# Loads by head pair, merged constants and a masked bounds matrix in a fused attention and FFN kernel

## The chip, the cores and the metric

The kernel runs on one core of one Trainium2 chip. The metric is the device time of one execution in microseconds (us). Several executions were timed for each kernel, and each comparison uses executions of both kernels on the same chip.

The engines are named as the profile names them: PE is TensorE (matmuls; PEld is its weight load), DVE is VectorE, ACT is ScalarE, POOL is GpSimd and SP is SyncE. In this kernel nearly all DMA transfers that load inputs are issued by POOL, and the issuing instruction occupies POOL.

## The reference, cut to what matters

For each of 4 batches and 8 heads there are 768 positions with head size 64. The keys come in 24 chunks of 32. For each query, an upper bound of the score with each chunk is computed from the chunk's smallest and largest keys; the six chunks with the largest bounds are kept, the others are masked; then comes ordinary causal attention, and a feed-forward network (FFN) with squared ReLU on the joined heads.

```python
k_min = np.min(k_chunks, axis=3); k_max = np.max(k_chunks, axis=3)
ub = np.sum(np.maximum(q * k_min, q * k_max), axis=-1)   # one bound per query and chunk (axes cut)
ub = np.where(causal, ub, -1e9)
top_chunks = np.argsort(ub, axis=-1)[..., -6:]
scores = np.where(selected & causal_by_position, scale * (q @ k.T), -1e9)
attn = softmax(scores)
x = (attn @ v)  reshaped to (3072, 512)
h = np.maximum(x @ w_in, 0.0)        # w_in 512 x 2048
out = (h * h) @ w_out                # w_out 2048 x 512
```

## The kernel before

Heads are worked in pairs, four pairs to a batch. A batch is worked in two *phases*, each for a block of 384 queries; there are eight phases. In each phase PE interleaves the attention of that block with the FFN of an earlier block. The FFN of a block can finish its sums only when all four pairs have written their part of `xT`, so the first phase has hardly any FFN work to fill PE with.

For each pair, stage A makes the transposed keys and queries, the chunk bounds and the selection:

```python
def stage_a(p, halves):
    ...
    for nm in ("k", "q"):
        pt = pool.tile([128, nt * QB], BF16, tag=tag, name=nm + "T")
        ...                                   # transposes on PE: kn, qn -> kT, qT in PSUM
        ops = kq if nm == "k" else qs
        for hh in range(2):
            rows = slice(D * hh, D * hh + D)
            nc.vector.tensor_copy(ops[s][hh][0:D, cols], pt[rows])      # kqc, qsc
        if nm == "k":
            kr = work.tile([128, 2, NC // 2 * nt], BF16, tag="kr", name="kr")
            ...                               # two tensor_reduce: max and min of each chunk
            for hh in range(2):
                rows = slice(D * hh, D * hh + D)
                nc.vector.tensor_copy(
                    kbd[s][rows, :, hh, 12 * n0:12 * n1], kr[rows])     # block-diagonal
            yield
    nc.vector.tensor_scalar_max(qp[:, 0:m], pt[:, u0 - QB * n0:], 0.0)
    nc.vector.tensor_scalar_min(qm[:, 0:m], pt[:, u0 - QB * n0:], 0.0)
    yield
    yield from selection(p, HT * n0, HT * n1, qp, qm)   # ub (PE), max8, selb (DVE), sT (PE), qsc (DVE)
```

Stage B makes the scores `ps` (PE), the exponentials `e` (ACT), the causal mask of `e` (POOL) and the products with the values `av` (PE). It ends in a serial chain:

```python
def finish():
    av = hold.pop("av")                       # PSUM, one buffer for each head of a pair
    for hh in range(2):
        nc.scalar.activation(rc[...], av[hh][...], ACT.Ln)
    nc.scalar.activation(rc, rc, ACT.Exp, scale=-1.0)
    for hh in range(2):
        nc.vector.tensor_mul(xTs[tb][rows, hp], av[hh][rows], rc[rows])
    ...
    if left[tb] == 0:
        ffn.extend(ffn_units(tb))
```

The loads of the first batch are in many pieces (half a sequence, one pair or several); those of later batches are one block of 768 KB each for keys, queries and values:

```python
load_qk(0, 0, 2, (0,), "k")
ident = ...; make_identity(nc, ident)
load_qk(0, 0, 2, (0,), "q")
load_qk(0, 2, H, (0,))
... # constants
load_v(0, 0)
load_w_in(0, 4)
...
put(0, 1, L(load_qk, 0, 0, H, (1,)), L(load_w_in, 4, NFI))
put(0, 2, L(load_v, 0, 1))
...
put(1, 0, L(load_qk, 1, 0, H), L(load_w_out), L(load_v, 1))
```

`put(ph, i, ...)` places work in phase `ph` before the stage B of its pair `i`. It is the order in which the program is written; the order on each engine is settled when the program is built.

The softmax here doesn't subtract the row's maximum and nothing guards it: scores larger than these inputs give would overflow.

Of the kernel before, what the change touches and what calls it, by code (L numbers as in the profile page):

```python
# [9 lines left out]
F32 = mybir.dt.float32  # L10
BF16 = mybir.dt.bfloat16
# [7 lines left out]
def kernel(  # L19
# [23 lines left out]
    NEG = -32768.0  # L43
    NP = H // 2
# [20 lines left out]
    def load_qk(b, h0, h1, halves=(0, 1), what="kq"):  # L65

        for nm, src in (("k", k), ("q", q)):
            if nm not in what:
                continue
            if (nm, b) not in nat:  # L70
                nat[nm, b] = ld.tile([128, H, NT, D], BF16, tag=nm + "n",
                                     name=nm + "n")
            j0, j1 = HT * halves[0], HT * (halves[-1] + 1)
            if j1 - j0 == NT:
                nc.gpsimd.dma_start(
                    out=nat[nm, b][:, h0:h1].rearrange("p h j d -> p (h j) d"),
                    in_=src[b, h0:h1].rearrange("h (j p) d -> p (h j) d",
                                                p=128))
                continue
            if h1 - h0 <= j1 - j0:  # L80
                for h in range(h0, h1):
                    nc.gpsimd.dma_start(
                        out=nat[nm, b][:, h, j0:j1],
                        in_=src[b, h, 128 * j0:128 * j1].rearrange(
                            "(j p) d -> p j d", p=128))
                continue
            for j in range(j0, j1):
                nc.gpsimd.dma_start(
                    out=nat[nm, b][:, h0:h1, j],
                    in_=src[b, h0:h1, 128 * j:128 * (j + 1)].rearrange(  # L90
                        "h p d -> p h d"))
# [5 lines left out]
    def load_v(b, half=None):  # L97

        if half is None:
            nc.gpsimd.dma_start(  # L100
                out=vo[b % 2][:, :, :, 0:D].rearrange("p h j d -> p (h j) d"),
                in_=v[b].rearrange("h (j p) d -> p (h j) d", p=128))
            return
        for j in range(HT * half, HT * half + HT):
            nc.gpsimd.dma_start(
                out=vo[b % 2][:, :, j, 0:D],
                in_=v[b, :, 128 * j:128 * (j + 1)].rearrange("h p d -> p h d"))

    load_qk(0, 0, 2, (0,), "k")
    ident = consts.tile([128, 128], BF16, tag="ident")  # L110
    make_identity(nc, ident)
    load_qk(0, 0, 2, (0,), "q")
    load_qk(0, 2, H, (0,))
# [3 lines left out]
    kq, qs, kbd, selb = [], [], [], []  # L117
    for s in range(NSET):
        kq.append([consts.tile([KC, S], BF16, tag=f"kq{s}{hh}", name="kqc")
                   for hh in range(2)])  # L120
        qs.append([consts.tile([KC, S], BF16, tag=f"qs{s}{hh}", name="qsc")
                   for hh in range(2)])
        kbd.append(consts.tile([128, 2, 2, NC], BF16, tag=f"kbd{s}", name="kbd"))
        selb.append(consts.tile([128, NT, 2, 32], BF16, tag=f"selb{s}",
                                name="selb"))

    def set_constants(s):
        nc.vector.memset(kbd[s], 0.0)
        for hh in range(2):
            nc.vector.memset(qs[s][hh][D:KC, 0:128], 0.0)  # L130
        nc.vector.memset(selb[s][:, :, :, NC:], 0.0)
        nc.vector.memset(selb[s][:, NT - 1], 0.0)
        for hh in range(2):
            if (s, hh) == (0, 0):
                nc.scalar.activation(
                    kq[0][0][D:KC, :].rearrange("c (a j) -> c a j", j=CH),
# [346 lines left out]
```

## Time and profile before

| | before |
|---|---|
| median of 3 runs | 330.38 us (330.23 to 330.52) |
| profiled span | 328.7 us |
| last `xT` of the first phase done | 41.56 us |
| PE idle in the first phase | 17.86 us |
| PE idle in phases 2 to 4 | 7.72 us |
| PE idle in phases 5 to 8 | 8.52 us |

The idle times are the length of a stretch less PE's busy time, from the busy time by stretch. These are that view's lines for the kernel before. The columns are the stretch, its length, busy us of PE, PEld, DVE, ACT and POOL (in brackets the instructions), the granted clock, the DMA engines' share and GB/s (the share is printed as the view gives it, also where it is above 1; nothing here rests on it). The first line is the first phase, the second is phases 2 to 4, the third the rest.

```profile
0.00:41.56 41.56, 23.70 (x144) 11.57 (x145) 34.97 (x137) 18.54 (x40) 34.22 (x62) 1.00 1.44 135
41.56:167.46 125.90, 118.18 (x928) 63.65 (x938) 104.25 (x317) 86.89 (x219) 37.34 (x84) 1.00 0.90 80
167.46:328.70 161.24, 152.72 (x1005) 83.47 (x1013) 79.88 (x224) 112.74 (x282) 27.54 (x92) 1.00 0.15 32
```

After 41.56 us PE is busy 94% of the time.

These are lines of DVE's timeline (start, duration, engine, line, operation, what it writes and reads, shapes, how many, and in brackets the idle time before and what ended it):

```profile
5.85 2.11 DVE L410 MEMSET vo<- 128x512 bf16 x4
7.97 0.72 DVE L201 COPY kqc<-kT 64x384 bf16<-64x384 bf16 x2
...
35.22 1.78 DVE L211 COPY kbd<-kr 64x24 bf16<-64x24 bf16 x2
...
41.00 0.56 DVE L369 TENSOR_TENSOR xT<-av_647,rc 64x384 bf16<-64x384 f32 x1
```

Constants keep DVE until 7.97 us, when the first key copy starts. At 35.22 us two tiny copies into `kbd` take 1.78 us together. The timeline of POOL shows what ran beside them, the block issues for the second batch, and behind these the issue of `w_out`:

```profile
34.62 2.23 POOL L75 DMA_DIRECT2D kn<-in_k_dram  x1
36.84 2.23 POOL L75 DMA_DIRECT2D qn<-in_q_dram  x1
39.04 1.18 POOL L176 DMA_DIRECT2D w_out_sb<-in_moe_w_out_dram  x1
```

Lastly PE's timeline: the first value products of pairs 0, 1 and 3 and the start of pair 3's scores (`ps`).

```profile
18.70 0.53 PE L345 MATMUL av_395<-e,vo 128*128 128x384 bf16 x1
...
29.25 0.53 PE L345 MATMUL av_488<-e,vo 128*128 128x384 bf16 x1
...
31.41 1.01 PE L379 MATMUL ps<-qsc,kqc 88*128 88x384 bf16 x3 [0.46 <-DVE qsc L254]
...
37.63 0.82 PE L345 MATMUL av_646<-e,vo 128*128 128x384 bf16 x3 [1.77 <-DVE xT L369]
```

Followed back, the chain that ended last in this kernel does not run through the last `xT` of the first phase. It leaves that phase at 34.62 us, over the two block issues shown above, and goes on over the load of `w_out` to the first product that uses it, for which PE stood idle 0.43 us (start, duration, what):

```profile
39.04 21.04 DMA w_out_sb<-in_moe_w_out_dram
60.12 0.39 PE py L302
```

### The profile page before, as it was taken

To read this page: it belongs to the slowest core of one execution; us is meant where nothing else is said; L and a number is where in the kernel's file an instruction comes from. 1 tells how busy PE (TensorE), PEld (TensorE's weight loads), DVE (VectorE), ACT (ScalarE), POOL (GpSimd) and SP (SyncE) were. 2 spreads that over 40 slices of the span, in tenths; PEclk is the share of its full clock that TensorE was granted. 3 is DMA by queue.
4 is the path that set the end of the run, shared out by engine and by line. 5 is a ranking of instruction groups with operands and counts; after the bars stand their busy time and mean duration, and the time that the engine had idled before them with its cause. 6 is when DMAs were issued, how large, how long until landed. Compare 5 with 4: busy or idle time off the path is not lost.

```text
span 328.7 us, 6090 instructions
## 1 busy us (share of the span) xinstructions
PE 294.6 (90%) x2076; PEld 158.7 (48%) x2096; DVE 219.1 (67%) x678; ACT 218.2 (66%) x540; POOL 99.1 (30%) x237
## 2 busy tenths in 40 slices
PE   1397699999998999999999999999999999999995
PEld 1143344454454445555455455554555555554542
DVE  7987879778899867999485488994576213421420
ACT  6064556786666559887479766787579679973731
POOL 8886840452410722202142222111122311210000
PEclk9999999999999999999999999999999999999999
DMA  6999999999590891000193010000100000001001
GB/s 45 151 148 195 134 159 210 119 127 98 60 102 3 56 194 40 2 1 3 41 101 52 2 66 32 2 1 3 64 34 0 32 34 32 2 0 64 35 33 64
DMA packets 81371, 20.87 MB, mean 63 GB/s; under 512 B 74836, under 2 KB 77756, under 8 KB 81340
## 3 DMA queue, kind: packets, MB, share of 16 engines
q0 software_dynamic: 77344, 13.63, 53.8%
q1 hardware_dynamic: 3996, 6.85, 5.6%
q8 instruction: 16, 0.26, 0.3%
q14 instruction: 15, 0.12, 0.1%
HBM read 27.26 MB, written 6.29 MB: 102 GB/s over the span
## 4 chain that ended last, share of the span: by engine, by line
PE 55%; DVE 24%; ACT 8%; DMA 6%; issue 3%; POOL 2%; ACTq 0%; DVEq 0%
PE py L302 21%; PE ph L288 13%; PE ps L379 8%; DMA w_out_sb<-in_moe_w_out_dram 6%; DVE kr L206 4%; ACT rc L359 4%; DVE xT L369 3%; DVE qsc L201 3%; ACT e L383 2%; DVE kqc L201 2%; PE sT L249 2%; DVE qsc L254 1%; ACT rc L362 1%; PE kT L194 1%; DVE qp L216 1%
## 5 line engine op out<-in xcount | busy, mean ns | idle before, releaser
L383 ACT ACTIVATE e<-ps 128x384 bf16<-128x384 f32 (+2 forms) x288 | 108.6, 430 | 37.1 <-PE ps L379 34.6
L386 POOL TENSOR_SCALAR_AFFINE_SELECT e<-e 128x128 bf16<-128x128 bf16 x192 | 55.9, 302 | 183.4 <-ACT e L383 181.6
L288 PE MATMUL ph<-xT,w_in_sb 128*128 128x384 bf16 x512 | 105.3, 331 | 4.8 <-ACT ht L293 3.0
L293 ACT ACTIVATE ht<-ph 128x384 bf16<-128x384 f32 x128 | 63.3, 503 | 22.6 <-PE ph L288 17.0
L379 PE MATMUL ps<-qsc,kqc 88*128 88x384 bf16 (+2 forms) x288 | 72.2, 303 | 6.2 <-ACT e L383 2.8
L288 PEld LDWEIGHTS <-w_in_sb 128*128 128x128 bf16 x512 | 48.7, 98 | 38.9 <-issue 13.4
L345 PEld LDWEIGHTS <-vo 128*128 128x128 bf16 x288 | 28.0, 101 | 20.9 <-DVE xT L369 3.2
L379 PEld LDWEIGHTS <-kqc 88*128 88x128 bf16 x288 | 27.2, 100 | 21.9 <-issue 5.7
L307 ACT COPY ob<-py 128x512 f32<-128x512 f32 x24 | 14.2, 590 | 25.7 <-PE py L302 25.5
L206 DVE TENSOR_REDUCE kr<-kT 128x24 bf16<-128x768 bf16 (+1 forms) x40 | 30.3, 793 | 0.3
L201 DVE COPY kqc<-kT 64x768 bf16<-64x768 bf16 (+1 forms) x40 | 18.9, 474 | 16.9 <-PE kT L194 16.3
L254 DVE COPY qsc<-sT 24x640 bf16<-24x640 bf16 (+2 forms) x40 | 16.7, 417 | 7.6 <-PE sT L249 6.8
L201 DVE COPY qsc<-qT 64x768 bf16<-64x768 bf16 (+1 forms) x40 | 18.9, 473 | 1.2 <-PE qT L194 0.6
L194 PE MATMUL kT<-ident,kn 128*64 128x128 bf16 x192 | 11.2, 240 | 8.7 <-POOL ident masks.py:199 4.3
L362 ACT ACTIVATE rc<-rc 128x384 f32<-128x384 f32 x32 | 16.5, 516 | 0.2
L194 PEld LDWEIGHTS <-kn 128*64 128x64 bf16 x192 | 6.8, 116 | 16.3 <-issue 6.5
L194 PE MATMUL qT<-ident,qn 128*64 128x128 bf16 x192 | 11.1, 237 | 1.5 <-DMA qn<-in_q_dram 1.3
L194 PEld LDWEIGHTS <-qn 128*64 128x64 bf16 x192 | 6.7, 114 | 9.6 <-DVE kr L206 4.3
L249 PE MATMUL sT<-ident,selb 128*128 128x128 bf16 x80 | 8.6, 233 | 2.7 <-DVE selb L241 2.4
L229 PE MATMUL ub<-kbd,qp 128*128 128x48 bf16 x80 | 7.7, 190 | 3.4 <-DVE qm L217 2.1
L211 DVE COPY kbd<-kr 64x48 bf16<-64x48 bf16 (+1 forms) x40 | 10.0, 251 | 0.5
L234 DVE TENSOR_TENSOR ubm<-ub,ubmask 128x240 f32<-128x240 f32 (+2 forms) x20 | 7.1, 353 | 4.5 <-PE ub L231 4.3
(648 smaller groups left out, 483.5 us busy)
## 6 DMA issues: line engine op xcount, KB each, us to landing
out_dram<-ob SPq DMA_DIRECT2D x24, 256.0 KB
kn<-in_k_dram POOLq DMA_DIRECT2D x3, 768.0 KB, 9.5
qn<-in_q_dram POOLq DMA_DIRECT2D x3, 768.0 KB, 11.6
vo<-in_v_dram POOLq DMA_DIRECT2D x3, 768.0 KB, 10.2
w_out_sb<-in_moe_w_out_dram POOLq DMA_DIRECT2D x1, 2048.0 KB, 21.0
w_in_sb<-in_moe_w_in_dram POOLq DMA_DIRECT2D x1, 1536.0 KB, 11.7
vo<-in_v_dram POOLq DMA_DIRECT2D x6, 128.0 KB, 7.3
kqc<-kqc SPq DMA_DIRECT2D x15, 36.0 KB
```

The costliest lines, as they stand in the source:

```text
L194: nc.tensor.matmul(pt[D * hh:D * hh + D, 128 * j:128 * (j + 1)], lhsT=nat[nm, b][:, 2 * hp + hh, n0 * HT + j], rhs=ident, is_transpose=Tru ...
L201: nc.vector.tensor_copy(ops[s][hh][0:D, cols], pt[rows])
L206: nc.vector.tensor_reduce(kr[:, mm], pt.rearrange("d (c j) -> d c j", j=CH), axis=AX.X, op=op)
L254: nc.vector.tensor_copy(qs[s][hh][D:KC, 128 * u0:128 * t1], sT[32 * hh:32 * hh + NC, :])
L288: nc.tensor.matmul(ph, lhsT=w_in_sb[:, ki, 128 * f:128 * (f + 1)], rhs=xT[:, ki], start=(ki == 0), stop=(ki == NKI - 1))
L293: nc.scalar.activation(ht, ph, ACT.Relu)
L302: nc.tensor.matmul(py, lhsT=h2[f][:, 128 * t:128 * (t + 1)], rhs=w_out_sb[:, f, :], start=(f == 0), stop=(f == NFI - 1))
L345: nc.tensor.matmul(hold["av"][hh][:, off:], lhsT=vo[b % 2].rearrange("p h n d -> p (h n d)")[:, c0:c0 + 2 * D], rhs=es[hh][:, off:], start ...
L362: nc.scalar.activation(rc, rc, ACT.Exp, scale=-1.0)
L379: nc.tensor.matmul(ps[:, off:], lhsT=kq[s][hh][:, 128 * j:128 * (j + 1)], rhs=qs[s][hh][:, q0 + off:q1], start=True, stop=True)
L383: nc.scalar.activation(e[:, off:], ps[:, off:], ACT.Exp, scale=scale)
L386: nc.gpsimd.affine_select(out=e[:, off:off + 128], in_=e[:, off:off + 128], compare_op=ALU.is_ge, fill=0.0, base=0, channel_multiplier=-1, ...
```

## The change

The intent is to shorten the start and to spare DVE. There are four parts:

1. **Loads.** Each load takes the whole sequence of one head pair (192 KB, one issue). Those of the first batch are issued early; those of later batches are spread, one pair at a time.
2. **Constants.** The tiles of all pairs are merged, so that one memset does what eight did. The ones in the values are written as 32-bit words.
3. **Bounds.** The two copies into the block-diagonal `kbd` become one multiply by a mask of heads.
4. **Query copies.** In the first phase ACT copies the queries, in place of DVE.

```diff
+    ONES = 1.0 + 0x3F80 / 2.0 ** 23
...
-    def load_qk(b, h0, h1, halves=(0, 1), what="kq"):
+    def load_qk(p, what="kq"):
+        b, h = p // NP, 2 * (p % NP)
...
+            nc.gpsimd.dma_start(
+                out=nat[nm, b][:, h:h + 2].rearrange("p h j d -> p (h j) d"),
+                in_=src[b, h:h + 2].rearrange("h (j p) d -> p (h j) d", p=128))
...                                            # load_v(p) likewise
-    load_qk(0, 0, 2, (0,), "k")
+    load_qk(0, "k")
     ident = consts.tile([128, 128], BF16, tag="ident")
     make_identity(nc, ident)
-    load_qk(0, 0, 2, (0,), "q")
-    load_qk(0, 2, H, (0,))
+    load_qk(0, "q")
+    load_qk(1)
...
+    own = consts.tile([128, 2], BF16, tag="own")
+    nc.vector.memset(own, 0.0)
+    for hh in range(2):
+        nc.vector.memset(own[D * hh:D * hh + D, hh:hh + 1], 1.0)
+    nc.vector.memset(kbds, 0.0)
+    nc.vector.memset(selbs[:, :, NT - 1], 0.0)
+    nc.vector.memset(selbs[:, :, 0:NT - 1, :, NC:], 0.0)
     for s in range(NSET):
...                                            # set_constants(s) removed
+        nc.vector.memset(qss[D:KC, s, :, 0:128], 0.0)
+    nc.vector.memset(vo[1].rearrange("p h j d -> p (h j) d").bitcast(F32)[
+        :, :, D // 2:], ONES)
...
-    load_v(0, 0)
+    load_v(0)
+    load_qk(2)
+    load_v(1)
+    load_qk(3)
     load_w_in(0, 4)
+    load_v(2)
+    load_v(3)
...
-                nc.vector.tensor_copy(ops[s][hh][0:D, cols], pt[rows])
+                if nm == "q" and first:
+                    nc.scalar.copy(ops[s][hh][0:D, cols], pt[rows])
+                else:
+                    nc.vector.tensor_copy(ops[s][hh][0:D, cols], pt[rows])
...
-                for hh in range(2):
-                    rows = slice(D * hh, D * hh + D)
-                    nc.vector.tensor_copy(
-                        kbd[s][rows, :, hh, 12 * n0:12 * n1], kr[rows])
+                nkc = NC // 2 * nt
+                nc.vector.tensor_mul(
+                    kbd[s][:, :, :, 12 * n0:12 * n1],
+                    kr.unsqueeze(2).to_broadcast([128, 2, 2, nkc]),
+                    own.unsqueeze(1).unsqueeze(3).to_broadcast(
+                        [128, 2, 2, nkc]))
...
-    put(0, 1, L(load_qk, 0, 0, H, (1,)), L(load_w_in, 4, NFI))
-    put(0, 2, L(load_v, 0, 1))
+    put(0, 2, L(load_w_in, 4, NFI))
     put(0, NP, ("A", 0, (1,), True))
+    put(0, NP, L(load_qk, NP), L(load_qk, NP + 1))
     for hp in range(1, NP):
         put(1, 0, ("A", hp, (1,), False))
-    put(1, 0, L(load_qk, 1, 0, H), L(load_w_out), L(load_v, 1))
+    put(1, 0, L(load_w_out))
...
-        if b + 1 < B:
-            put(e + 1, 1, L(load_qk, b + 1, 0, H))
-            put(e + 1, NP, L(load_v, b + 1))
+    for hp in range(2, NP):
+        put(1, hp - 1, L(load_qk, NP + hp))
+    for hp in range(NP):
+        put(1, hp, L(load_v, NP + hp))
+        for b in range(2, B):
+            put(NBLK * b - 2, hp, L(load_qk, NP * b + hp))
+            put(NBLK * b - 1, hp, L(load_v, NP * b + hp))
```

More of the change, by code (lines that the diff above doesn't have):

```diff
@@ L72, in load_qk @@
                                      name=nm + "n")
-            j0, j1 = HT * halves[0], HT * (halves[-1] + 1)
-            if j1 - j0 == NT:
-                nc.gpsimd.dma_start(
-                    out=nat[nm, b][:, h0:h1].rearrange("p h j d -> p (h j) d"),
-                    in_=src[b, h0:h1].rearrange("h (j p) d -> p (h j) d",
-                                                p=128))
-                continue
-            if h1 - h0 <= j1 - j0:
-                for h in range(h0, h1):
-                    nc.gpsimd.dma_start(
-                        out=nat[nm, b][:, h, j0:j1],
-                        in_=src[b, h, 128 * j0:128 * j1].rearrange(
-                            "(j p) d -> p j d", p=128))
-                continue
@@ L87, in load_qk @@
-            for j in range(j0, j1):
-                nc.gpsimd.dma_start(
-                    out=nat[nm, b][:, h0:h1, j],
-                    in_=src[b, h0:h1, 128 * j:128 * (j + 1)].rearrange(
-                        "h p d -> p h d"))
+            nc.gpsimd.dma_start(
+                out=nat[nm, b][:, h:h + 2].rearrange("p h j d -> p (h j) d"),
+                in_=src[b, h:h + 2].rearrange("h (j p) d -> p (h j) d", p=128))
     vo = [consts.tile([128, H, NT, 2 * D], BF16, tag=f"vo{s}", name="vo")
@@ L95 @@
           for s in range(2)]
-    def load_v(b, half=None):
-        if half is None:
-            nc.gpsimd.dma_start(
-                out=vo[b % 2][:, :, :, 0:D].rearrange("p h j d -> p (h j) d"),
-                in_=v[b].rearrange("h (j p) d -> p (h j) d", p=128))
-            return
-        for j in range(HT * half, HT * half + HT):
-            nc.gpsimd.dma_start(
-                out=vo[b % 2][:, :, j, 0:D],
-                in_=v[b, :, 128 * j:128 * (j + 1)].rearrange("h p d -> p h d"))
@@ L109, with load_v @@
-    load_qk(0, 0, 2, (0,), "k")
+    def load_v(p):
+        b, h = p // NP, 2 * (p % NP)
+        nc.gpsimd.dma_start(
+            out=vo[b % 2][:, h:h + 2, :, 0:D].rearrange("p h j d -> p (h j) d"),
+            in_=v[b, h:h + 2].rearrange("h (j p) d -> p (h j) d", p=128))
+    load_qk(0, "k")
     ident = consts.tile([128, 128], BF16, tag="ident")
     make_identity(nc, ident)
-    load_qk(0, 0, 2, (0,), "q")
-    load_qk(0, 2, H, (0,))
+    load_qk(0, "q")
+    load_qk(1)
     NSET = 2 * NP
-    kq, qs, kbd, selb = [], [], [], []
@@ L118 @@
-    for s in range(NSET):
-        kq.append([consts.tile([KC, S], BF16, tag=f"kq{s}{hh}", name="kqc")
-                   for hh in range(2)])
-        qs.append([consts.tile([KC, S], BF16, tag=f"qs{s}{hh}", name="qsc")
-                   for hh in range(2)])
-        kbd.append(consts.tile([128, 2, 2, NC], BF16, tag=f"kbd{s}", name="kbd"))
-        selb.append(consts.tile([128, NT, 2, 32], BF16, tag=f"selb{s}",
-                                name="selb"))
-    def set_constants(s):
-        nc.vector.memset(kbd[s], 0.0)
-        for hh in range(2):
-            nc.vector.memset(qs[s][hh][D:KC, 0:128], 0.0)
-        nc.vector.memset(selb[s][:, :, :, NC:], 0.0)
-        nc.vector.memset(selb[s][:, NT - 1], 0.0)
-        for hh in range(2):
-            if (s, hh) == (0, 0):
-                nc.scalar.activation(
-                    kq[0][0][D:KC, :].rearrange("c (a j) -> c a j", j=CH),
-                    ident[0:NC, 0:NC].unsqueeze(2).to_broadcast([NC, NC, CH]),
-                    ACT.Copy, scale=NEG)
-            else:
-                nc.sync.dma_start(out=kq[s][hh][D:KC, :], in_=kq[0][0][D:KC, :])
@@ L142 @@
-    set_constants(0)
-    set_constants(1)
+    kqs = consts.tile([KC, NSET, 2, S], BF16, tag="kqs", name="kqc")
+    qss = consts.tile([KC, NSET, 2, S], BF16, tag="qss", name="qsc")
+    selbs = consts.tile([128, NSET, NT, 2, 32], BF16, tag="selbs", name="selb")
+    kbds = consts.tile([128, NSET, 2, 2, NC], BF16, tag="kbds", name="kbd")
+    kbd = [kbds[:, s] for s in range(NSET)]
+    kq = [[kqs[:, s, hh] for hh in range(2)] for s in range(NSET)]
+    qs = [[qss[:, s, hh] for hh in range(2)] for s in range(NSET)]
@@ new lines, with kq_rows @@
+    selb = [selbs[:, s] for s in range(NSET)]
+    def kq_rows(i):
+        dst = kqs[D:KC, i // 2, i % 2]
+        if i == 0:
+            nc.scalar.activation(
+                dst.rearrange("c (a j) -> c a j", j=CH),
+                ident[0:NC, 0:NC].unsqueeze(2).to_broadcast([NC, NC, CH]),
+                ACT.Copy, scale=NEG)
+        else:
+            nc.sync.dma_start(out=dst, in_=kqs[D:KC, 0, 0])
+    own = consts.tile([128, 2], BF16, tag="own")
+    nc.vector.memset(own, 0.0)
+    for hh in range(2):
+        nc.vector.memset(own[D * hh:D * hh + D, hh:hh + 1], 1.0)
@@ L144 @@
+    nc.vector.memset(kbds, 0.0)
+    nc.vector.memset(selbs[:, :, NT - 1], 0.0)
+    nc.vector.memset(selbs[:, :, 0:NT - 1, :, NC:], 0.0)
+    for s in range(NSET):
+        nc.vector.memset(qss[D:KC, s, :, 0:128], 0.0)
+    nc.vector.memset(vo[1].rearrange("p h j d -> p (h j) d").bitcast(F32)[
+        :, :, D // 2:], ONES)
+    for i in range(2 * NP):
+        kq_rows(i)
     for j in range(2):
@@ L188, in stage_a @@
         m = QB * n1 - u0
-        pool, tag = (psf, "ff") if p < NP and n1 == 1 else (pst, "tp")
+        first = p < NP and n1 == 1
+        pool, tag = (psf, "ff") if first else (pst, "tp")
         for nm in ("k", "q"):
@@ L200, in stage_a @@
                 rows = slice(D * hh, D * hh + D)
-                nc.vector.tensor_copy(ops[s][hh][0:D, cols], pt[rows])
+                if nm == "q" and first:
+                    nc.scalar.copy(ops[s][hh][0:D, cols], pt[rows])
+                else:
+                    nc.vector.tensor_copy(ops[s][hh][0:D, cols], pt[rows])
             if nm == "k":
@@ L208, in stage_a @@
                         axis=AX.X, op=op)
-                for hh in range(2):
-                    rows = slice(D * hh, D * hh + D)
-                    nc.vector.tensor_copy(
-                        kbd[s][rows, :, hh, 12 * n0:12 * n1], kr[rows])
+                nkc = NC // 2 * nt
[4 more added lines that the diff above has]
+                        [128, 2, 2, nkc]))
                 yield
@@ L424 @@
         put(e + 1, 0, ("A", p0 + NP - 1, (0, 1), False))
-        if b + 1 < B:
-            put(e + 1, 1, L(load_qk, b + 1, 0, H))
-            put(e + 1, NP, L(load_v, b + 1))
-    phases[0][1:1] = [L(set_constants, 2), L(set_constants, 3)]
-    for ss in range(NP, NSET):
-        put(1, 1, L(set_constants, ss))
-    for j in range(NT):
-        put(1, j // 2 + 1, L(nc.vector.memset, vo[1][:, :, j, D:], 1.0))
+    for hp in range(2, NP):
[5 more added lines that the diff above has]
+            put(NBLK * b - 1, hp, L(load_v, NP * b + hp))
+    for i in range(2 * NP, 2 * NSET):
+        put(1, 1, L(kq_rows, i))
     for ph, items in enumerate(phases):
```

## The prediction

> **What bounds the kernel now.** From about 42 us to the end it is bound by TensorE: in the table of busy time by stretch, PE is busy 270.9 of 287.1 us (94%). The first 41.6 us are different: PE is busy 23.7 us and DVE 35.0 us. Between 8 and 31.6 us DVE hardly rests; each of the four first query/key stages costs it about 5 us. So the start is a DVE chain, and the FFN, which fills PE later, can start only when xT of the fourth head pair is done (41.56 us in the timeline). That moment is what the change can move.
>
> **What the change removes, adds and moves (durations from the groups by form and the timeline).**
> 1. Constants. Before the first key copy DVE runs memsets until 7.97 us, though the first key transposes are done at 5.4 us; the largest are the vo memsets, 485 ns each for 512 bf16 (five before the copy, a sixth at 9.8 us). Afterwards vo is one memset of 1536 f32 words, 1.6 us by the same rate of one element per cycle. This agrees with the Trainium skill, "VectorE: DVE Perf Modes", section on zero memsets as uint32: a cycle per element whatever the type. I estimate the new list at 4.9 us, ending near 5.7 us. The first key load is now whole-sequence, 192 KB, one issue; I estimate about 1.03 us of issue (0.78 us for 3 blocks, 2.23 us for 48) and landing near 5.1 us. Net: first key copy about 2.2 us earlier.
> 2. First query copies: 8 x 353 ns leave DVE for ACT, which is idle until 16.8 us. 0.7 us per stage.
> 3. Bounds: two kbd copies (175 ns each undisturbed) become one tensor_mul of about 0.25 us. The copies sometimes stall: 1.78 us for two at 35.2 us, while POOL issues a DMA. The Trainium skill, "SBUF — State Buffer", section "Who interferes with whom", says SBUF-to-SBUF copies in a two-port mode share ports with GpSimd exclusively, and that tensor_tensor does not fight descriptor writing. This trace agrees on the copies. Worth about 0.3 us per stage and 1.5 us at the stall.
> 4. Loads: 48 issues of about 1.03 us instead of 2.23 us blocks and many small ones. More POOL time (about +10 us), and POOL is blocked by issuing until about 17 us, so the first masks of e come at about 17 us, as before. w_out is issued about 5 us earlier.
>
> **On the critical path.** Stepping the new DVE order with these durations, the fourth stage's last scores start near 25 us instead of 31.4, and the last xT of the first phase ends near 34 us instead of 41.6. I expect the gain of 7.5 us to survive, because PE work after that is unchanged; the DVE-bound stretch 100 to 140 us gains at most 0.15 us per stage.
>
> **Time.** 330.4 - 7.5 = 322.9 us; 8 times in 10 between 319.5 and 326.8. Chances: faster by over 2% (below 323.8) 0.57, within 2% 0.42, slower by over 2% 0.01.
>
> **What would show it.** First key copy on DVE at 5.5 to 6 us; kbd multiply near 0.25 us, not stretched under POOL issues; first exponential near 13.5 us (was 16.8); first phase's last xT near 34 us; PE busy total still about 295 us.
>
> **What would make it wrong.** Loads for pairs 2 and 3 landing late (they queue behind values and second halves): then PE waits on kn at 15 to 20 us and the gain halves. POOL's masks delaying the first value products. w_out landing after it is needed. DVE becoming the limit in the second phase, so that the early gain is absorbed. A broadcast multiply much slower than 0.25 us.

## More of the kernel before

Because `av` has one buffer for each head, the value products of a pair wait for the `xT` of the pair before.

In the first phase DVE has more work than PE, 34.97 us against 23.70. What PE waited for there is in the table of waits (waited for by whom, us in total, times, longest us):

```profile
PE kT L194 <- POOL ident masks.py:199: 4.3, 1, 4.3
PE kT L194 <- DVE kr L206: 3.3, 2, 2.6
PE ps L379 <- DVE qsc L254: 2.0, 3, 1.0
PE av_646 L345 <- DVE xT L369: 1.8, 1, 1.8
```

Apart from the start itself, all of these are waits for DVE; the same table has 1.9 us more in which PE waited for loads of keys and queries.

## The result, and the profile after

| | before | after |
|---|---|---|
| median of 4 runs | 330.43 us (330.23 to 330.52) | 326.12 us (325.48 to 326.29) |
| ratio, with its 95% interval | 1 | 0.9867 (0.985 to 0.9884) |
| profiled span | 328.7 us | 324.3 us |
| last `xT` of the first phase done | 41.56 us | 40.66 us |
| PE idle, first phase | 17.86 us | 17.50 us |
| PE idle, phases 2 to 4 | 7.72 us | 4.19 us |
| PE idle, phases 5 to 8 | 8.52 us | 7.99 us |

A ratio here and below is the mean time of one kernel's fast runs over that of the other's of the same rounds, so it is not quite the ratio of the quoted medians. The change is a gain of 1.3%, within 2%, and both kernels are correct.

The page's busy times of the kernel after (share of the span, number of instructions):

```profile
PE 294.6 (91%) x2096; PEld 158.9 (49%) x2096; DVE 207.9 (64%) x619; ACT 221.1 (68%) x548; POOL 110.0 (34%) x254
```

PE's work was 294.6 us before as well, so the 4.4 us between the spans are all PE idle time. (The trace before holds 2076 matmul records and this one 2096, so idle times are known to some tenths of a us and no better.) The busy time by stretch of the kernel after says where they lie:

```profile
0.00:40.66 40.66, 23.16 (x147) 11.33 (x148) 27.79 (x100) 22.03 (x48) 28.43 (x55) 1.00 1.57 146
40.66:163.07 122.41, 118.22 (x935) 63.97 (x935) 100.73 (x299) 86.41 (x219) 54.56 (x109) 1.00 0.94 85
163.07:324.30 161.23, 153.24 (x1015) 83.62 (x1013) 79.41 (x221) 112.66 (x282) 27.02 (x90) 1.00 0.08 28
```

Compare with the same view before. In the first phase DVE lost 7.2 us of work (34.97 to 27.79), but the phase became only 0.9 us shorter. Phases 2 to 4 became 3.5 us shorter. The prediction had it the other way round.

The first part went as planned. These are DVE's lines after:

```profile
3.77 1.34 DVE L128 MEMSET vo<- 128x1536 f32 x1 [0.37 <-issue]
6.07 0.72 DVE L198 COPY kqc<-kT 64x384 bf16<-64x384 bf16 x2 [0.96 <-PE kT L188]
...
40.09 0.56 DVE L368 TENSOR_TENSOR xT<-av_585,rc 64x384 bf16<-64x384 f32 x1
```

The first key copy starts 1.9 us earlier (7.97 to 6.07), after DVE has already waited 0.96 us for the transposes. The first exponential starts at 14.73 us (16.84 before). Then most of the gain is lost. PE's timeline, the first value products of each of the four pairs and the start of pair 3's scores:

```profile
22.10 0.53 PE L344 MATMUL av_336<-e,vo 128*128 128x384 bf16 x1
...
27.00 0.80 PE L344 MATMUL av_426<-e,vo 128*128 128x384 bf16 x3 [0.59 <-POOL e L385]
27.59 0.53 PE L378 MATMUL ps<-qsc,kqc 88*128 88x384 bf16 x1
...
32.38 0.80 PE L344 MATMUL av_470<-e,vo 128*128 128x384 bf16 x3 [1.09 <-DVE xT L368]
...
36.09 0.80 PE L344 MATMUL av_584<-e,vo 128*128 128x384 bf16 x3 [1.06 <-DVE xT L368]
```

The last scores start 3.8 us earlier than before (31.41 to 27.59). But the first value products come 3.4 us later (18.70 to 22.10), and from there three more pairs have to go through the chain of products, `rc` and `xT`, one after the other. Those of pair 1 still come 2.2 us earlier than before (29.25 to 27.00), those of pair 3 only 1.5 us (37.63 to 36.09). So not all is lost before pair 1: for instance, pair 1's `rc` was ready at 30.27 us, but DVE first copied and reduced keys for the next phase and began `xT` at 31.68. From the last scores to the last `xT` it now takes 40.66 - 27.59 = 13.07 us, 2.9 us more than before.

POOL's timeline has a new thing in it: the first masks follow an issue without a pause.

```profile
14.21 2.10 POOL L85 DMA_DIRECT2D vo<-in_v_dram  x2
16.36 1.54 POOL L385 TENSOR_SCALAR_AFFINE_SELECT e<-e 128x128 bf16<-128x128 bf16 x6
```

So POOL was issuing up to 16.3 us, while the first exponentials had run since 14.73. The six masks of pair 0 were done at 17.90 us. That its value products came only at 22.10 us is PE's order: in the built program they stand behind the transposes of pair 2's selection, which ran at 21.91 us. And PE's waits in the first phase are of another kind than before:

```profile
PE kT L188 <- DMA kn<-in_k_dram: 8.2, 4, 5.5
PE sT L248 <- DVE selb L240: 3.5, 4, 1.7
PE av_470 L344 <- DVE xT L368: 1.1, 1, 1.1
PE av_584 L344 <- DVE xT L368: 1.1, 1, 1.1
```

Of the 8.2 us for `kn`, 5.5 are the very start, where the kernel before waited 4.3 us for POOL's `ident`; the rest are three waits for later keys. The loads of 192 KB come in one after the other, most of them 1 to 2 us after the last. The keys of pair 3 landed at 18.17 us. The chain that ended last, followed back and given here in order of time from 11 us on (start, duration, what), runs over that load and then over the chain of value products:

```profile
11.47 6.70 DMA kn<-in_k_dram
18.22 0.42 PE kT L188 x3
...
27.00 0.80 PE av_426 L344 x3
...
31.68 0.56 DVE xT L368
```

Two links of that view have to be read with care, because releasers are inferred. As what released pair 1's products at 27.00 us it gives POOL's masks of 25.88. Counted off in sixes, these are pair 2's masks, and pair 1's were done at 22.16 us. What had just ended was the first half of pair 0's `xT`:

```profile
26.30 0.55 DVE L368 TENSOR_TENSOR xT<-av_336,rc 64x384 bf16<-64x384 f32 x1
```

It ended at 26.85, 0.15 us before, and the products of pairs 2 and 3 also start 0.14 to 0.15 us after such an `xT`. So pair 1 too most likely waited for the one buffer. And before the `xT` at 31.68 us the view gives an exponential, where DVE itself was busy with keys until then.

In phases 2 to 4 two waits of PE for DVE disappeared. Before, that table had these lines, and after it has none for `qm`, nor one of the scores `ps` for `qsc`:

```profile
PE ub L229 <- DVE qm L217: 1.9, 4, 0.7
PE ps L379 <- DVE qsc L254: 0.7, 1, 0.7
```

(The table of that stretch also has 1.6 us of an FFN product waiting for `xT`. But that product starts at 41.61 us, so its wait is the end of the first phase and is no part of the 7.72 us.) `w_out` changed its place too: it now lands at 51.80 us instead of 60.08, is first used at 69.41 us, and is not on the chain that ended last any more.

### The profile page after: what moved, and what is told of

The parts are those of the page before. It is cut to its first block, busy times and chain, and to the rows that moved or that the text cites. A ratio compares the mean times of both kernels' runs of the same rounds, so it can differ in the third digit from the quotient of the medians.

```text
span 324.3 us, 6103 instructions
## 1 busy us (share of the span) xinstructions
PE 294.6 (91%) x2096; PEld 158.9 (49%) x2096; DVE 207.9 (64%) x619; ACT 221.1 (68%) x548; POOL 110.0 (34%) x254
## 2 busy tenths in 40 slices
DMA packets 81642, 20.86 MB, mean 64 GB/s; under 512 B 75108, under 2 KB 78028, under 8 KB 81612
## 4 chain that ended last, share of the span: by engine, by line
PE 66%; DVE 17%; ACT 7%; issue 3%; POOL 3%; DMA 2%; POOLq 0%; ACTq 0%
PE py L301 23%; PE ph L287 18%; PE ps L378 9%; DVE xT L368 3%; ACT rc L358 3%; DVE qsc L198 3%; PE kT L188 2%; DMA kn<-in_k_dram 2%; DVE kr L203 2%; PE sT L248 2%; ACT e L382 2%; ACT ht L292 1%; PE qT L188 1%; ACT rc L361 1%; DVE qp L215 1%
## 5 line engine op out<-in xcount | busy, mean ns | idle before, releaser
L382 ACT ACTIVATE e<-ps 128x384 bf16<-128x384 f32 (+2 forms) x288 | 111.4, 431 | 34.7 <-PE ps L378 33.2
L385 POOL TENSOR_SCALAR_AFFINE_SELECT e<-e 128x128 bf16<-128x128 bf16 x192 | 57.0, 305 | 167.4 <-ACT e L382 165.8
L85 POOL DMA_DIRECT2D vo<-in_v_dram x16 | 16.5, 1039 | 6.9 <-PE ps L378 6.9
L188 PE MATMUL kT<-ident,kn 128*64 128x128 bf16 x192 | 10.9, 239 | 8.7 <-DMA kn<-in_k_dram 8.2
L198 DVE COPY qsc<-qT 64x768 bf16<-64x768 bf16 (+1 forms) x32 | 16.1, 503 | 3.7 <-PE qT L188 3.3
L75 POOL DMA_DIRECT2D kn<-in_k_dram x16 | 16.6, 1036 | 2.0 <-PE ps L378 1.2
L75 POOL DMA_DIRECT2D qn<-in_q_dram x16 | 16.4, 1027 | 0.2
L188 PE MATMUL qT<-ident,qn 128*64 128x128 bf16 x192 | 10.3, 237 | 1.3 <-DMA qn<-in_q_dram 1.0
```

What stands on the lines that cost most here:

```text
L75: nc.gpsimd.dma_start(out=nat[nm, b][:, h:h + 2].rearrange("p h j d -> p (h j) d"), in_=src[b, h:h + 2].rearrange("h (j p) d -> p (h j) d" ...
L188: nc.tensor.matmul(pt[D * hh:D * hh + D, 128 * j:128 * (j + 1)], lhsT=nat[nm, b][:, 2 * hp + hh, n0 * HT + j], rhs=ident, is_transpose=Tru ...
L382: nc.scalar.activation(e[:, off:], ps[:, off:], ACT.Exp, scale=scale)
L385: nc.gpsimd.affine_select(out=e[:, off:off + 128], in_=e[:, off:off + 128], compare_op=ALU.is_ge, fill=0.0, base=0, channel_multiplier=-1, ...
```

## The experiments

Twelve runs were made, one of them of the changed kernel itself, all correct, each against the kernel before on the same chip. The medians of the kernel before were 330.25, 329.65, 330.37 and 330.09 us in the four sets, so a ratio is the safer number. Except where said, each edit is made to the kernel after.

Two readings stood against each other. One: the new loads fill POOL and the DMA engines at the start and cost more than they bring. The other: the new loads bring a good part of the gain, elsewhere.

### Query copies back on DVE

```diff
-                if nm == "q" and first:
+                if False:
                     nc.scalar.copy(ops[s][hh][0:D, cols], pt[rows])
```

> The changed kernel with the first query copies back on DVE. Theory (the copies on ACT freed DVE time, 0.7 us in each of four stages, that was on the chain): 2 to 3 us slower, 328 to 329 us. Rival (the trace shows qp on DVE waiting for ACT's copy of the same qT, so the time was only moved into a wait, and the first phase ends on the chain of value products anyway): within 0.7 us of the changed kernel, 325.5 to 326.8 us.

Measured: 325.8 us (325.02 to 326.79), ratio 0.9865 (0.9843 to 0.9887). That is the time of the kernel after. In the changed kernel as it stands, moving these copies to ACT is worth nothing measurable. The first phase of this profile even ended at 39.47 us. DVE's table of waits in the kernel after shows that the move has a price of its own:

```profile
DVE qp L215 <- ACT qsc L196: 1.5, 3, 0.7
```

DVE's `qp` reads the same PSUM tile as ACT's copy, and in the built program it waits for that copy, three times, 1.5 us in all.

### Bounds by two copies again

```diff
-                nkc = NC // 2 * nt
-                nc.vector.tensor_mul(...)     # kr times own, broadcast
+                for hh in range(2):
+                    rows = slice(D * hh, D * hh + D)
+                    nc.vector.tensor_copy(
+                        kbd[s][rows, :, hh, 12 * n0:12 * n1], kr[rows])
```

> The changed kernel with the two kbd copies back in place of the multiply by the head mask. Theory (the copies stall while POOL writes descriptors, and the second to fourth phases, where DVE is busiest, lose time by it): 1.5 to 3 us slower, 327.5 to 329 us, with single copies of 1 us or longer in the trace beside POOL issues. Rival (only the undisturbed cost counts, 0.15 us a stage): within 0.7 us.

Measured: 326.92 us (326.23 to 328.36), ratio 0.9903 (0.9877 to 0.9929). By the ratios the multiply is worth about 1.2 us, but the interval overlaps that of the kernel after (0.985 to 0.9884), so this is weak. These are the lines of the tile `kbd` of the kernel before, the kernel after and this one (number, then duration in ns as smallest, median and largest, first and last start, forms):

```profile
L211 DVE COPY kbd<-kr x40: 102/175/1599, 10.2 to 236.8; 64x48 bf16<-64x48 bf16 x24, 64x24 bf16<-64x24 bf16 x16
```

```profile
L207 DVE TENSOR_TENSOR kbd<-kr,own x20: 199/254/360, 7.9 to 232.1; 128x96 bf16<-128x96 bf16 x12, 128x48 bf16<-128x48 bf16 x8
```

```profile
L208 DVE COPY kbd<-kr x40: 159/174/659, 7.9 to 234.7; 64x48 bf16<-64x48 bf16 x24, 64x24 bf16<-64x24 bf16 x16
```

The multiply costs what was predicted and is never stretched beyond 360 ns. With the copies back but the small issues kept, the worst copy takes 659 ns, not 1599. So part of what the multiply was meant to cure is already cured by the shorter issues.

### All loads as before

```diff
-    def load_qk(p, what="kq"):
+    def load_qk(b, h0, h1, halves=(0, 1), what="kq"):
...            # load_qk, load_v, and every place where they are issued, as in the kernel before
```

> The changed kernel with the loads as before (half sequences first, whole batches later). Theory A (the whole-sequence loads cost the first phase: PE waits 2.7 us for kn of pairs 1 to 3 and POOL issues until 16.3 us before it masks the first e): faster, 323 to 325 us, the first phase's last xT before 39 us. Theory B (the gain of the second to fourth phases comes from the loads: w_out lands at 51.8 us, not 60.1, and keys of the second batch arrive by pair): slower, 328 to 330 us, though the first phase ends earlier.

Measured: 328.41 us (327.86 to 328.59), ratio 0.994 (0.9925 to 0.9954). The loads are worth 2.4 us of the 4.4 (0.994 less 0.9867, times 330). The reading that they cost more than they bring fell. In this profile the first value products come at 17.62 us, before even those of the kernel before, and yet the first phase ends at 42.00 us (theory B had it end earlier) and `w_out` lands at 58.93 us (51.80 in the kernel after, 60.08 before).

### Constants as before

```diff
-    nc.vector.memset(kbds, 0.0)
...
+    def set_constants(s):
+        nc.vector.memset(kbd[s], 0.0)
...            # as in the kernel before, with the six memsets of vo in phase 1
```

> The changed kernel with the constants as before (64 small memsets and six of vo). Theory (the first key copy goes back to about 8 us and all of the first phase shifts by it): 1.5 to 2.5 us slower, 327.6 to 328.6 us. Rival (the loads of pairs 1 to 3 set the pace of the first phase, the memsets end before they matter): within 0.7 us.

Measured: 327.62 us (327.0 to 327.8), ratio 0.9912 (0.9896 to 0.9929). The merged constants are worth 1.5 us. The first key copy of this profile starts at 8.59 us and the first phase ends at 41.80 us. The four undone parts add up to 0 + 1.2 + 2.4 + 1.5 = 5.1 us, close to the whole gain of 4.4.

### Only the first batch's loads as before

```diff
+    def load_qk_o(b, h0, h1, halves=(0, 1), what="kq"):      # the old load_qk; load_v_o likewise
...
-    load_qk(0, "k")
+    load_qk_o(0, 0, 2, (0,), "k")
...
-    put(0, 2, L(load_w_in, 4, NFI))
+    put(0, 1, L(load_qk_o, 0, 0, H, (1,)), L(load_w_in, 4, NFI))
+    put(0, 2, L(load_v_o, 0, 1))
```

> The changed kernel with the first batch's loads as before and only the later batches by head pair. With all loads as before it was 328.4 us, against 326.1. Theory (the 2.3 us come from the later loads: second-batch keys and queries in two pairs let w_out be issued and land 7 us earlier and leave POOL free): 326 to 327 us, w_out landed by 53 us. Rival (they come from the first batch's loads, fewer POOL issues between the masks of the first phase): 328 to 329 us.

Measured: 327.25 us (326.81 to 328.14), ratio 0.9928 (0.9902 to 0.9954); the first phase ends at 41.82 us and `w_out` lands at 52.93 us. The time lies between what the theory and the rival said.

### Only the later batches' loads as before

```diff
-    put(0, NP, L(load_qk, NP), L(load_qk, NP + 1))
...
-    put(1, 0, L(load_w_out))
+    put(1, 0, L(load_qk_o, 1, 0, H), L(load_w_out), L(load_v_o, 1))
...
+        if b + 1 < B:
+            put(e + 1, 1, L(load_qk_o, b + 1, 0, H))
+            put(e + 1, NP, L(load_v_o, b + 1))
```

> The complement: first batch's loads by head pair as in the changed kernel, later batches in whole-batch blocks as before. Theory (later loads): 327.8 to 328.8 us, w_out landing near 58 us, second-phase value products near 59 us instead of 49 us. Rival (first batch's loads): 326 to 326.7 us.

Measured: 326.91 us (326.46 to 327.34), ratio 0.9918 (0.9894 to 0.9943). `w_out` lands at 56.49 us. This time too lies between theory and rival. The first phase ends at 40.21 us, no later than in the kernel after; by this one profile the loss is in the phases behind it, where PE idles 1.59, 3.29 and 1.30 us in the second, third and fourth phase, against 0.83, 2.45 and 0.93 in the kernel after. (That is weak: 9 of the trace's matmul records are missing there, and a second profile of the kernel after, below, has 4.62 us in these phases, where this one has 6.18 and the first had 4.19.) Undoing either half of the loads gives back 1.7 to 2.0 us, and undoing both 2.4 us, so the halves do not add.

### Keys first, the rest behind the first masks

The values of later pairs and `w_in` are not needed at once. This kernel issues keys and queries of pairs 2 and 3 with only the first values between them, and everything else later.

```diff
-    load_v(0)
     load_qk(2)
-    load_v(1)
+    load_v(0)
     load_qk(3)
-    load_w_in(0, 4)
-    load_v(2)
-    load_v(3)
...
-    put(0, 2, L(load_w_in, 4, NFI))
+    put(0, 1, L(load_v, 1), L(load_w_in, 0, 4))
+    put(0, 2, L(load_v, 2), L(load_v, 3), L(load_w_in, 4, NFI))
```

> The changed kernel with only the order of the first loads changed: keys and queries of pairs 2 and 3 before the values of pairs 1 to 3 and the first quarter of w_in, which are issued among the masks of the first phase. Theory (the first phase is paced by loads landing about 1.5 us apart, k of pair 3 at 18.2 us, and by POOL issuing until 16.3 us before the first mask): k of pair 3 lands near 16 us, the first value product is at 18 to 19 us instead of 22.1, the first phase's last xT at 38 to 39 us instead of 40.7, and the time 324 to 325 us. Rival (the first phase ends on the serial chain of normalisation over one value buffer, whatever the loads do): first phase's end and time within 0.7 us of the changed kernel.

Measured: 322.39 us (321.23 to 322.58), ratio 0.977 (0.9744 to 0.9795): faster than the kernel before by 2.3%, and it beats both kernels. Its first phase, in the busy time by stretch (columns as above):

```profile
0.00:37.93 37.93, 22.20 (x153) 11.34 (x155) 28.30 (x102) 21.93 (x49) 28.46 (x55) 0.81 1.57 147
```

The first phase is 2.7 us shorter than in the kernel after (37.93 against 40.66). This is so although the granted clock was 0.81 in this stretch of this execution. PE idles 15.73 us there instead of 17.50. POOL's and PE's timelines of this kernel: pair 0's masks with the issue between them, pair 0's value products, and the start of pair 3's scores:

```profile
15.56 0.29 POOL L381 TENSOR_SCALAR_AFFINE_SELECT e<-e 128x128 bf16<-128x128 bf16 x1 [3.01 <-ACT e L378]
16.00 1.03 POOL L85 DMA_DIRECT2D vo<-in_v_dram  x1
17.04 1.29 POOL L381 TENSOR_SCALAR_AFFINE_SELECT e<-e 128x128 bf16<-128x128 bf16 x5
```

```profile
15.90 0.48 PE L340 MATMUL av<-e,vo 128*128 128x384 bf16 x1
...
17.43 1.22 PE L340 MATMUL av<-e,vo 128*128 128x384 bf16 x5
...
26.72 1.01 PE L374 MATMUL ps<-qsc,kqc 88*128 88x384 bf16 x3 [0.47 <-DVE qsc L249]
```

POOL is idle for 3.01 us and masks as soon as the first exponential is there. The first value product comes at 15.90 us instead of 22.10. Note the end of pair 0, though: its last mask was done at 18.33 us, later than in the kernel after (17.90), and yet its last product was done at 18.65 us, where the kernel after needed until 23.58.

### The same with the query copies on DVE

The edit is that of the first experiment, made to the kernel of the last one.

```diff
-                if nm == "q" and first:
+                if False:
```

> The same, with the first query copies on DVE. Putting them back alone changed nothing (325.8 us), though the first phase ended 1.2 us earlier. Theory (qp and qm wait for ACT's copies of the same qT, 1.5 us of DVE idle in the first phase): first phase's last xT before 38.5 us, time 323.5 to 325 us. Rival: as the run with the copies on ACT, within 0.7 us.

Measured: 324.43 us (323.93 to 325.02), ratio 0.984 (0.9817 to 0.9863), on the same chip as the last one. With this order of loads the copies on ACT are worth about 2 us (324.43 - 322.39), and the intervals do not overlap. In the order of the change as made they were worth nothing. Why is not shown: the first phase of this profile ends at 38.66 us, only 0.7 us later than in the last one, and the rest of the loss lies in phases 2 to 4, where the edit changes no instruction.

### The changed kernel again

No edit: the same program once more, on another chip, beside the next two.

> The changed kernel unchanged, as the base of this call: 325.5 to 326.5 us.

Measured: 325.98 us (324.26 to 328.61), ratio 0.9853 (0.9823 to 0.9882). The eight runs of the changed kernel spread over 4.35 us (324.26 to 328.61). The kernel before, over all its runs, spread over 1.64 us (329.03 to 330.67). The profiled execution was the slowest, and its stretches show where it differs:

```profile
0.00:42.40 42.40, 23.14 (x147) 11.35 (x148) 27.67 (x100) 22.12 (x48) 28.61 (x55) 1.00 1.51 141
42.40:165.67 123.27, 118.65 (x927) 64.37 (x935) 100.77 (x299) 86.66 (x219) 54.57 (x109) 1.00 0.93 84
```

The same program, at the same clock, needs 42.40 us for its first phase here and 40.66 us in the first profile, with equal work on the engines. The keys of pairs 1, 2 and 3 landed at 10.39, 14.95 and 19.93 us here and at 9.20, 13.68 and 18.17 us there. The other 0.9 us lie in phases 2 to 4. So a first-phase gain of 0.9 us is one draw out of a spread, and the first-phase ends that this document takes from single profiles are known to some 1.7 us and no better. (The faster order of loads stands out of this: its three kernels end the first phase at 37.93, 38.66 and 38.35 us, the kernels that issue all the small loads ahead of the first masks at 39.47 to 42.40.) And the gain in phases 2 to 4 is there in both profiles (2.6 and 3.5 us).

### Only the order of the loads

Keys and queries of pair 3 before the second values, as in the faster kernel, but everything still issued before the first masks.

```diff
-    load_v(0)
     load_qk(2)
-    load_v(1)
+    load_v(0)
     load_qk(3)
+    load_v(1)
     load_w_in(0, 4)
```

> The changed kernel with k2, q2, v0, k3, q3, v1 in this order and all loads still issued ahead of the first mask. It keeps POOL busy issuing to 16.3 us and moves only the landing of keys and queries of pairs 2 and 3. Theory A (the landing of keys paced the first phase): about all of the 3.7 us that the later order gained, 322 to 323.5 us. Theory B (POOL being free for the first masks gave it, by letting the value products start at 16 us and not at 22): little, 325 to 326.3 us, the first value product still after 21 us.

Measured: 325.45 us (324.76 to 325.88), ratio 0.9852 (0.9836 to 0.9868), the same as the changed kernel beside it. The keys of pair 3 landed at 16.59 us, as early as in the faster kernel (16.74 us). But the first mask came at 16.38 us, and PE's first value products stand where they stood in its order (the second line is the start of pair 3's scores):

```profile
21.21 1.49 PE L344 MATMUL av<-e,vo 128*128 128x384 bf16 x6
...
26.66 0.52 PE L378 MATMUL ps<-qsc,kqc 88*128 88x384 bf16 x1
```

So the earlier landing of the keys alone brings nothing measurable in the time, though this profile's first phase ended at 39.72 us. Its last scores start when those of the faster kernel do (26.66 and 26.72 us), but from there to the last `xT` it takes 13.06 us and in the faster kernel 11.21. What remains of the faster kernel is that POOL masks earlier and that the value products come earlier. The order on PE is settled when the program is built, and in the faster kernel the first of the value products stands ahead of the transposes of pair 1's selection, where in the changed kernel all of them stand behind those of pair 2's. No run changed one of the two alone. But the traces speak for PE's order as the nearer cause: pair 0's masks were all done by 17.98 us here and by 17.90 in the kernel after, before the 18.33 of the faster kernel, and the products were done 4 to 5 us later all the same (22.70 and 23.58 us against 18.65).

### The faster kernel without the wait of `qp` for ACT

```diff
-                if nm == "q" and first:
-                    nc.scalar.copy(ops[s][hh][0:D, cols], pt[rows])
-                else:
+                if nm == "k" or not first:
                     nc.vector.tensor_copy(ops[s][hh][0:D, cols], pt[rows])
...
         nc.vector.tensor_scalar_min(qm[:, 0:m], pt[:, u0 - QB * n0:], 0.0)
+        if first:
+            for hh in range(2):
+                nc.scalar.copy(qs[s][hh][0:D, cols],
+                               pt[D * hh:D * hh + D])
```

> The faster order of loads (322.4 us), with ACT's copies of the first queries emitted after the two DVE operations that read the same qT. Theory (DVE idles in the first phase because qp waits for ACT's copies, which the program orders first, though neither writes what the other reads): those waits are gone, the first phase ends 0.5 to 1.5 us earlier than 37.9 us, and the time is 321 to 322 us. Rival (the first phase is paced by loads and by the chain of value products): within 0.7 us of 322.4 us, waits moved to ACT and PE.

Measured: 322.4 us (321.26 to 322.76), ratio 0.9756 (0.9734 to 0.9778). The time is that of the faster kernel, and the first phase ends at 38.35 us, not earlier. The run could not test the theory, though: in the faster kernel DVE's table has no wait of `qp` for ACT to begin with (the 1.5 us were those of the kernel after), so there was none to remove.

### Later batches' loads as before, but the values later

This is the kernel "only the later batches' loads as before" with one load moved. The theory was that the block issue of the second batch's values holds POOL's masks up in the second phase. Five rounds.

```diff
-    put(1, 0, L(load_qk_o, 1, 0, H), L(load_w_out), L(load_v_o, 1))
+    put(1, 0, L(load_qk_o, 1, 0, H), L(load_w_out))
+    put(1, 2, L(load_v_o, 1))
```

> The kernel with the later loads in whole-batch blocks (326.9 us, 0.9918 of the kernel before), with one thing changed: the second batch's value load is emitted after the second score stage of the second phase, so that POOL makes the first masks of that phase before it writes this load's descriptors; w_out is issued and lands as late as there. Theory (a POOL issue ahead of the first masks of a phase puts its value products late, at 57 us in place of 49, in the order that is fixed at build): the first value product of the second phase near 50 us, and the ratio back at 0.985 to 0.988. Rival (the lateness of w_out, 56 to 58 us, or of the second batch's keys costs it): ratio 0.990 to 0.993, as before this edit.

Measured: 327.99 us (327.53 to 328.37), ratio 0.9937 (0.9923 to 0.995). It did not get faster, so the theory fell; the ratio is near what the rival said. The first value products of the second phase did come earlier (52.99 against 57.13 us), and `w_out` landed as late as without the edit (56.52 us); here it was first used at 69.90 us, and PE did not wait for it. By what way the small later loads save PE's idle time in phases 2 to 4 stays open; the order on the engines is built anew with each such edit, so these kernels differ in more than the load.

## Why the prediction was right or wrong, point by point

**The time and the range.** 322.9 us was predicted, 326.12 came. The range (319.5 to 326.8) holds it, near its upper end. The gain was 4.3 us where 7.5 were expected, and the likeliest of the named classes, faster by over 2%, did not come. That the time fell inside the range is in good part luck: the first phase, from which all of the 7.5 us were to come, became 0.9 us shorter in one profile and 0.8 us longer in the other, and most of what came is from phases for which almost nothing was forecast.

**What bounds the kernel: right for the later phases.** PE's work stayed at 294.6 us and the gain is PE idle time only. But that the last `xT` of the first phase is the moment that counts was taken as given, while the chain that ended last ran past it over the load of `w_out` (39.04 to 60.08 us).

**Constants: nearly right.** The first key copy was put at 5.5 to 6 us; it came at 6.07. The value memset was put at 1.6 us and took 1.34. Undoing the part costs 1.5 us.

**Query copies: the cost right, the worth wrong in this order of loads.** They were counted as 0.7 us a stage. Undone, they change nothing; in the faster kernel they are worth 2 us.

**Bounds: right on the cost.** 254 ns was measured for 0.25 us predicted, and the worst was 360 ns. The worth is about 1.2 us, weakly shown. That the long copies come with block issues agrees with the runs: with the small issues the worst copy fell from 1599 to 659 ns. The page "SBUF — State Buffer" of the Trainium skill, section "Who interferes with whom", explains such stretching by an exclusive port pair; the runs agree with it but do not test the mechanism.

**Loads: the cost right, their effect misplaced.** Each issue took 1.03 us, and POOL's busy time rose by 10.9 us where 10 were predicted. `w_out` was issued 3.0 us earlier (39.04 to 36.08) where 5 were predicted, and landed 8.3 us earlier.

**The critical path: wrong, and this is the step that failed.** The prediction stepped DVE's order alone. It said "the fourth stage's last scores start near 25 us" and "the last xT of the first phase ends near 34 us". They came at 27.59 and 40.66 us (42.40 in the second profile). Two terms were too small:

- The scores. Of the 6.4 us expected, 3.8 came. The first exponential was 1.2 us later than predicted (14.73 against 13.5), and the chain then runs over the load of pair 3's keys, which landed at 18.17 us. The prediction named late keys as a danger. But landing them at 16.59 us by order alone did not shorten the kernel, so this was not the whole of it.
- The tail. The prediction left 9 us from the last scores to the last `xT` (34 - 25). It was 10.15 us in the kernel before, as its timeline already said, and 13.07 in the kernel after. In the prediction's words, "POOL is blocked by issuing until about 17 us, so the first masks of e come at about 17 us, as before". The masks came at 16.36, so the fact was right. The prediction even named masks that delay the first value products among the dangers, but its sum has no term for them. After the change the exponentials were ready sooner, at 14.73 us, and the masks came straight behind the issues. The value products of pair 0 came later still, at 22.10 us, behind pair 2's selection in PE's order, which a stepping of DVE alone could not see; and three more pairs queued behind one buffer. The faster kernel shows that this can be undone: issue less before the first masks, and the first value product comes at 15.90 us and the kernel is 3.2 us faster than the changed one in the same chip's comparison (0.9756 for its variant against 0.9853, times 330). The order of the keys alone was shown not to do it. POOL's time and the built order on PE were not told apart by a run; the traces point to the order on PE, since pair 0's masks were done earlier in the slower kernel (17.90 us) than in the faster one (18.33).

**Later phases: wrong in the other direction.** "PE work after that is unchanged" is true, and from it the prediction concluded that hardly anything after the first phase would change ("at most 0.15 us per stage"). But PE idled 7.72 us in phases 2 to 4, with 1.9 us waiting for `qm` and 0.7 us for `qsc` in the table of waits, and DVE had 3.5 us less to do there. PE's idle time fell by 3.5 us (3.1 in the second profile). This unforeseen gain makes up most of what was won, and hides much of what the first phase failed to give. Undoing the later loads alone costs 1.7 us, and its one profile shows it in those phases; the exact path is open.

## What to carry to other kernels

When a bottleneck at the start is taken away, step all the engines of the chain to its end, not the relieved engine alone: an engine that issues transfers "until the same time as before" can become a delay once its input is ready earlier, and the order in which the program is built on each engine can hold back work whose data are ready (here pair 0's masks were done at 17.90 us and its products came at 22.10). Look at that order in the trace after the change. Try to issue first what the first work needs, and to leave the rest until the engine that issues has done its first useful work; in this kernel that was worth 3.2 us, where the order of the loads alone was worth nothing measurable. By which way it acted is not fully shown. And count the idle time of the bounding engine in every stretch before calling a stretch unchanged: 94% busy over 287 us still left 16 us.

## What the Trainium skill lacked or had wrong

- "VectorE: DVE Perf Modes", section "Zero memsets can be issued as uint32 (trn2)": a cycle per element whatever the type. The trace agrees in kind: 512 bf16 elements took 485 ns, 384 uint32 words 378 ns and 1536 f32 words 1.34 us. From the first and the last, an element costs 0.835 ns and an instruction some 57 ns besides, which also gives the 378 ns. The section names no such fixed part. The prediction's 1.6 us for 1536 words means 1.04 ns a word, so its miss lies in the time per element and not in the fixed part.
- "DMA: Bandwidth & Descriptors", section "Anatomy of one DMA — SWDGE (gpsimd) path": its fit of 2.0 us plus bytes over 436e3 gives an estimate of 2.45 us for 192 KB (196,608 bytes). The first such load took 4.1 us from issue to landing (the smallest of all loads of keys in the first 45 us; the next loads were already issued behind it), and in a train the median was 5.2 us for keys. The section "Specifications" of the same page names 512 bytes as the smallest transfer for the full rate; in the kernel after 75,108 of 81,642 packets are below that, and from 8 to 18 us the DMA engines move only 157 to 186 GB/s (in windows of 1 us; up to 18 us, 1.92 of 2.32 MB were loads issued by POOL). That agrees with the page, but no run changed the packet size.
- No page gives in figures how long POOL is held by an issue according to its form. The traces show 0.78 us for 3 blocks of 128 rows, 1.03 us for 12 and 2.23 us for 48, so some 0.03 us for each block and 0.7 us for the issue. This set when POOL was free for its first mask.
- No page says how far the times of one program may spread at the same clock: the changed kernel's eight runs spread by 4.35 us, where the kernel before spread by 1.64 us over all its runs. In the two profiles of the changed kernel the keys of pair 3 landed at 18.17 and 19.93 us; that the train of loads makes the spread is not shown.
